# Making the parts of the down weights: spacing, early loads, and the queue of their stores

## The chip, the cores and the metric

The kernel runs on one core of one Trainium2 chip. The metric is the device time of one execution in microseconds (us), the median of several runs. The core has a matrix engine (PE, its weight loads shown as PEld), a vector engine (DVE), a scalar engine (ACT), GpSimd (POOL) and SyncE (SP). SP computes nothing here; it issues transfers. Transfers that POOL issues go through a queue that the profile calls q0 (software_dynamic), those of SP through q1 (hardware_dynamic). All engines take their instructions in order, and wait for each other through semaphores.

## The reference

One transformer block in float32 over 2048 tokens of width 576, with a batch of one:

```
h   = x + attention(layernorm(x))        32 heads of width 18, one shared key and value head
out = h + ((ln(h) Wg) * (ln(h) Wu)) Wd   hidden width 4608, no nonlinearity on either branch

scores = q k^T * 18^-0.5 ; p = softmax(scores) ; o = p v ; attention = o Wo
```

## The kernel before, in words

**Numbers in two parts.** Products are computed to nearly float32 precision from operands that are split into a high part (a cast to a reduced float32 format) and a low part (the rest): three products, high by high, high by low and low by high, are summed in PSUM.

**The stages.** Tokens are taken in four blocks of 512. At first all keys, values and the first queries are made (`keys_values`). Then comes a loop that this document calls the query loop (lines 952 to 962). Each of its steps issues two pairs of score tiles (`pair`: two matmuls on line 500, and one exponential of 128x1024 elements on ACT on line 501), and beside them PE makes the remaining queries of all blocks (`queries`, matmuls on line 337). The rate is 3 units of query work per step; a query of seven heads is 13 units of one and one of four. A head group of four heads takes 16 steps; at its end DVE copies the sums of its values out of PSUM (line 516), and PE can begin the next group's sums only when that bank is empty. The queries of block 0 and their bounds are followed by those of blocks 1 to 3. Each finished query goes through five DVE instructions (lines 344 to 349) and is stored to DRAM through SP (lines 351 and 352); the group after the present one is read back through SP (`prefetch_q`, line 424), from the third tile of a group on.

After the query loop, `steps` goes on with score tiles alone until 208 pairs are made, `load_wo_0` loads and splits the output weights (POOL casts on line 87, DVE subtracts on line 88), block 0 of the residual is loaded, and the first group ends at a guard that all engines pass. The feed-forward part follows, in which later attention runs beside the gate, up and down products.

**The down weights' parts.** The product with the down weights uses seven products of half-size blocks where eight would be needed, and so needs sums of the weights' blocks, each in two parts. `down_weights` makes these once, for 18 pairs of 128-row tiles, and stores them to `wd_dram`; the feed-forward part reads them back many times. It is a generator: the query loop calls it once per step, at the step's end, after `pair`, `run_aux` and `flush`. For a pair p that begins at step `begin(p)`, relative to that step it gives out:

| step | what | engine, line |
|---|---|---|
| -2 | `load`: four blocks, 576 KB | POOL queue, 874 |
| 0 and 1 | `sums`: two subtractions each, 128x288 | POOL, 880 |
| 2 | `high`: two casts, 128x864 and 128x1152 | POOL, 888 |
| 4 and 5 | `low`: one subtraction each, in place | DVE, 894 |
| 6 | `store`: high part and low part, 1008 KB each | POOL queue, 900 |

The last pair (17) has no sums and is stored as it is, in two parts. Within one step, work of a lower pair comes first, and for one pair the order is store, load, sums, high, low.

Each pair lives in a room, two buffers of 128x8x288 elements. Pairs 0 to 9 use two rooms in turn, pairs 10 to 17 three. Rooms come from memory that other tiles have left: the two first residual buffers, the buffer of a block's attention output (pairs 1 and 3), and the normalised inputs of blocks 0 and 1 when their queries are done (`XT0` from pair 5, `XT1` from pair 10). A load waits until the store of the pair that had the room before has landed. The order on every engine is the order of the program text (a manual schedule); a step is a place in that order and not a point in time. An engine whose inputs are there runs ahead of the others.

Pairs 0 to 10 begin six steps apart and the later ones four steps apart:

```
return 2 + 6 * min(p, 10) + 4 * max(p - 10, 0)
```

Of the kernel before, what the change touches and what calls it, by code (L numbers as in the profile page):

```python
# [32 lines left out]
NC = NF // 2  # L33
# [24 lines left out]
class Block:  # L58
# [780 lines left out]
            if not self.half and len(self.pend) > keep:  # L839
                self.flush(len(self.pend) - keep)  # L840

    def steps(self, on):

        while on():
            self.pair()
            self.pair()
            self.run_aux(1)
            self.flush(len(self.pend) - 1)

    def down_weights(self):  # L850

        pool, dve = self.nc.gpsimd, self.dve
        rooms = [(self.hp.tile([P, 8, HD], F32, tag="h", name="wd_src"), self.hp.tile([P, 8, HD], F32R, tag="h", name="wd_hi"))]
        at, where = {}, {}

        def begin(p):
            return 2 + 6 * min(p, 10) + 4 * max(p - 10, 0)  # L860

        def room(p):
            n = p % 2 if p < 10 else (2, 0, 1)[(p - 10) % 3]
            if p in (1, 5, 10):
                home, tag = {1: (self.otp, "oT"), 5: (self.p0q, "XT0"), 10: (self.p0q, "XT1")}[p]
                if p > 1:
                    self.XT[p // 5 - 1] = None
                e = home.tile([P, 9 * TB], F32R, tag=tag, name=f"wd_room{p}").rearrange("p (k j d) -> p k j d", k=2, d=HD)
                rooms[n:] = [(f32(e[:, 0]), e[:, 1])]
            return rooms[n]  # L870

        def load(p):
            where[p] = room(p)
            pool.dma_start(where[p][0][:, 0:4], self.wd[p])

        def sums(p, i):
            src, _ = where[p]
            if p < NC - 1:
                for i, x, y in ((4, 0, 1), (5, 3, 4), (6, 3, 0), (7, 2, 5))[i:i + 2]:
                    pool.tensor_tensor(src[:, i], src[:, x], src[:, y], ALU.subtract)  # L880

        def spans(p):
            return [(1, 4), (4, 8)] if p < NC - 1 else [(0, 4)]

        def high(p):
            src, hi = where[p]
            for lo, to in spans(p):
                pool.tensor_copy(hi[:, lo:to], src[:, lo:to])

        def low(p, i):  # L890

            src, hi = where[p]
            for lo, to in spans(p)[i:i + 1]:
                dve.tensor_tensor(src[:, lo:to], src[:, lo:to], f32(hi[:, lo:to]), ALU.subtract)

        def store(p):
            src, hi = where.pop(p)
            lo, to = spans(p)[0][0], spans(p)[-1][1]
            for k, t in enumerate((f32(hi), src)):
                pool.dma_start(self.wd_dram[p, :, 0:to - lo, k], t[:, lo:to])  # L900
            if p == 3:
                del rooms[1]

        for p in range(NC):
            for d, f in ((6, lambda p=p: store(p)), (-2, lambda p=p: load(p)), (0, lambda p=p: sums(p, 0)), (1, lambda p=p: sums(p, 2)),
                         (2, lambda p=p: high(p)), (4, lambda p=p: low(p, 0)), (5, lambda p=p: low(p, 1))):
                at.setdefault(begin(p) + d, []).append(f)
        for k in range(max(at) + 1):
            for f in at.pop(k, ()):
                f()  # L910
            yield

    def run(self):
        from contextlib import ExitStack
        tc = self.tc
        self.q_dram = tc.dram_tile([NB, H * DH, 3, TB], F32, name="q_dram")
        self.wd_dram = tc.dram_tile([NC, P, 7, 2, HD], F32, name="wd_dram")
        self.wd_list = [(b, p, j) for b in range(NB) for p in range(NC) for j in (range(4) if p == NC - 1 else ORDER)]
        self.n_wd = 0
        self.m_dram = tc.dram_tile([NB, 2, H, TB], F32, name="m_dram")  # L920
        self.known, self.n_mx, self.os, self.chunks = [0] * NB, 0, {}, []
        self.h, self.qt, self.normed, self.wr, self.ws, self.wdo, self.wo_r, self.wos = {}, {}, {}, {}, {}, {}, {}, {}
        self.n_pair, self.half, self.pend, self.aux, self.round = 0, [], [], [], 0
        self.tqs = []
        self.p2, self.p_next, self.wo_from, self.due = None, -1, 10 ** 6, 0.0
        with ExitStack() as st:
            pool = lambda name, bufs, **k: st.enter_context(tc.tile_pool(name=name, bufs=bufs, **k))
            cp, self.lp, self.hp = pool("const", 1), pool("ln", 2), pool("resid", 2)
            self.qp, self.pp, self.op, self.otp = pool("q", 2), pool("P", P_BUFS), pool("o", 1), pool("oT", 1)
            self.ps = pool("ps", 1, space=PSUM)  # L930
            self.C = cp.tile([P, C_W], F32, name="C")
            self.ident = self.C[:, C_ID:C_ID + P]
            self.kT = cp.tile([P, S], F32R, name="kT")
            self.V = cp.tile([P, NT, 32], F32, name="V")
            self.G = cp.tile([P, 64], F32R, name="G")
            self.mx = cp.tile([H, 8], F32, name="mx")
            st.enter_context(tc.manual_schedule())
            with tc.tile_pool(name="p0q", bufs=1) as self.p0q:
                self.wq_h = self.p0q.tile([P, 5, D], F32R, name="wq_h")
                self.wq_l = self.p0q.tile([P, 5, D], F32R, name="wq_l")  # L940
                self.XT = [self.p0q.tile([P, 9, TB], F32R, tag=f"XT{b}", name=f"XT{b}") for b in range(NB)]
                with tc.tile_pool(name="qb", bufs=2) as self.qb:
                    first = self.keys_values()
                    work = self.down_weights()

                    def rest():
                        yield from first
                        for b in range(1, NB):
                            yield from self.queries(b)
                    self.cast = self.dve.tensor_copy  # L950
                    others, live, due = rest(), True, 0.0
                    while live:
                        self.pair()
                        due += RATE
                        while due > 0 and live:
                            z = next(others, None)
                            live = z is not None
                            due -= z or 0
                        self.pair()
                        self.run_aux(1)  # L960
                        self.flush(len(self.pend) - 1)
                        next(work, None)
                    drain(work)
            self.flag()
            self.wp, self.hh, self.p2 = pool("w", 2), pool("hid", 4), pool("P2", 1)
            self.steps(lambda: self.n_pair < WO_FROM)
            self.load_wo_0()
            self.load_x(0)
            self.steps(lambda: self.n_pair % (2 * NT))
            self.flush(len(self.pend))  # L970
            self.guard()
            self.wo_from = self.n_pair + 12
            self.steps(lambda: self.more(0))
            self.cast = self.act.copy
            self.load_w(0)
            self.load_w(1)
            self.load_wd(WD_BUFS - NQ)
            self.load_x(1)
            self.fill(2.0, 1)
            while 0 not in self.normed:  # L980
                self.run_aux(1)
                self.fill(1.0, 1)
            self.split_w(0)
            while self.n_pair % 8 != 4:
                self.pair()
                if not self.half:
                    self.flush(len(self.pend) - 1)
            self.flush(len(self.pend))
            self.normal(0)
            for _ in range(2):  # L990
                self.pair()
            for i, _ in enumerate(self.spread(0)):
                if i % 2 == 0:
                    self.pair()
            self.flush(len(self.pend))
            del self.oT
            self.room()
            self.load_wd(WD_BUFS)
            for b in range(NB):
                self.ffn(b)  # L1000
# [10 lines left out]
WO_FROM = 208  # L1011
# [24 lines left out]
def f32(ap):  # L1036
    return ap.bitcast(F32)
# [10 lines left out]
def drain(gen):  # L1048
    for _ in gen:
        pass  # L1050
# [69 lines left out]
```

## Time and profile before

| what | us |
|---|---|
| median of three runs | 2411.1 |
| lowest and highest | 2410.78, 2415.26 |
| the profiled execution | 2413.92 |
| its span, first to last instruction | 2412.0 |
| PE busy in the span | 2335.0 |
| ACT busy | 1432.2 |
| DVE busy | 1160.4 |
| POOL busy | 669.4 |

The mean granted clock of PE is 0.988 of full speed. A row of the timeline gives the start in us from the span's start, the duration, the engine, the line of the kernel, the operation, the tile written and the tiles read, the shapes and, in brackets, how long the engine was idle before it and what ended that. A row of waits gives the waiting engine and line, the releaser, the total in us, the number of times and the longest. In a row of windows, the stretch and its length stand first, then for PE, PEld, DVE, ACT and POOL the busy time with the number of instructions, and then the granted clock, the busy share of the DMA engines and GB/s.

### The profile page before, as it was taken

Reading aid. Unit: us, or ns where it says so; the run is one execution under the profiler, and the core shown is the slowest. Engines: PE = TensorE matmul, PEld = TensorE weight load, DVE = VectorE, ACT = ScalarE, POOL = GpSimd, SP = SyncE. Lnnn points to the kernel's source line nnn. Section 1 sums busy time; section 2 is a strip of 40 time slices with the busy share of each in tenths; the row PEclk is TensorE's granted clock in tenths of the full one; section 3 lists DMA queues with packets and bytes.
Section 4 is the critical chain, followed back from the end, with each engine's and each line's share of the span. In section 5 each row is a group of like instructions: output and inputs, shape, how many; then the busy total and the mean of one; then the engine's idle time right before and its main releaser. Section 6 shows DMA issues by size and latency. Waiting matters only on the chain.

```text
span 2412.0 us, 46184 instructions
## 1 busy us (share of the span) xinstructions
PE 2335.0 (97%) x18425; PEld 1623.5 (67%) x18425; DVE 1160.4 (48%) x2142; ACT 1432.2 (59%) x1857; POOL 669.4 (28%) x827
## 2 busy tenths in 40 slices
PE   6999888999999999999999999999999999999999
PEld 4434324567677766767767667676766688888887
DVE  7545433444343434543434345443434376566565
ACT  4877666766666666566676766656666623232332
POOL 3655510022222222112222222212221233233332
PEclk9999998999999999999999999999999999999999
DMA  4676752333333333533333333453333344655553
GB/s 138 217 253 224 233 179 92 102 121 108 120 116 121 110 117 104 167 107 116 121 117 121 117 112 111 131 158 116 101 118 108 109 163 163 202 180 190 172 168 119
DMA packets 130467, 340.21 MB, mean 141 GB/s; under 512 B 14760, under 2 KB 15528, under 8 KB 130248
## 3 DMA queue, kind: packets, MB, share of 16 engines
q1 hardware_dynamic: 119208, 290.31, 37.7%
q0 software_dynamic: 11040, 46.89, 5.8%
q8 instruction: 147, 2.41, 0.4%
q14 instruction: 72, 0.59, 0.1%
HBM read 272.63 MB, written 55.67 MB: 136 GB/s over the span
## 4 chain that ended last, share of the span: by engine, by line
PE 81%; DVE 1%; ACT 1%; DMA 1%; issue 0%; SPq 0%; POOL 0%; ACTq 0%; POOLq 0%
PE y L746 17%; PE pg L786 16%; PE acc L505 15%; PE gu L786 12%; PE s L500 9%; PE pu L786 9%; PE yo L616 2%; PE y L734 1%; PE pt L543 1%; ACT P L501 1%; PE to L136 0%; DVE h L749 0%; DMA X<-X 0%; PE tx L665 0%; DMA out_dram<-h 0%
## 5 line engine op out<-in xcount | busy, mean ns | idle before, releaser
L501 ACT ACTIVATE P<-s 128x1024 f32<-128x1024 f32 x1024 | 1030.0, 1027 | 370.8 <-PE s L500 291.1
L786 PE MATMUL pg<-X,ws 64*128 64x512 f32 x2565 | 705.8, 392 | 0.0
L786 PE MATMUL pu<-X,ws 64*128 64x512 f32 x2565 | 705.5, 392 | 0.0
L754 POOL TENSOR_TENSOR h<-h,tmp 128x288 f32<-128x288 f32 x408 | 318.6, 810 | 920.2 <-ACT tmp L753 919.2
L786 PEld LDWEIGHTS pg<-X,ws 64*128 64x128 f32 x2565 | 474.5, 186 | 66.7 <-issue 4.5
L505 PE MATMUL acc<-P,V 128*32 128x512 f32 x4096 | 495.7, 603 | 9.2 <-DVE os L516 8.5
L786 PEld LDWEIGHTS pu<-X,ws 64*128 64x128 f32 x2565 | 472.2, 186 | 31.9
L500 PE MATMUL s<-q,kT 56*128 56x512 f32 x2048 | 440.5, 426 | 14.0 <-DMA q<-q_dram 9.0
L746 PEld LDWEIGHTS y<-wdo,room 128*128 128x128 f32 x2856 | 386.1, 188 | 49.4 <-issue 45.8
L746 PE MATMUL y<-wdo,room 128*128 128x288 f32 x2856 | 404.3, 300 | 1.3 <-DVE h L749 1.2
L753 ACT COPY tmp<-y 128x288 f32<-128x288 f32 x408 | 162.9, 400 | 327.3 <-PE y L746 322.0
L749 DVE TENSOR_TENSOR h<-h,y 128x288 f32<-128x288 f32 x544 | 236.0, 454 | 243.1 <-PE y L746 240.3
L500 PEld LDWEIGHTS s<-q,kT 56*128 56x128 f32 x2048 | 196.1, 186 | 213.0 <-ACT P L501 107.9
L786 PE MATMUL gu<-X,ws 64*128 64x512 f32 x2646 | 309.1, 389 | 0.3 <-DMA X<-X 0.2
L87 POOL CAST ws<-wr 128x1152 fp32r<-128x1152 f32 x144 | 165.8, 1151 | 493.1 <-PE pu L786 239.0
L505 PEld LDWEIGHTS acc<-P,V 128*32 128x32 f32 x4096 | 114.7, 109 | 258.8 <-issue 242.4
L786 PEld LDWEIGHTS gu<-X,ws 64*128 64x128 f32 x2646 | 250.6, 184 | 51.5 <-issue 4.2
L808 DVE TENSOR_TENSOR hf<-pu,g 128x512 f32<-128x512 f32 x95 | 65.7, 692 | 356.1 <-ACT g L804 356.1
L88 DVE TENSOR_TENSOR ws<-wr,ws 128x1152 fp32r<-128x1152 f32 x144 | 194.9, 1353 | 63.6 <-POOL ws L87 63.6
L88 DVE TENSOR_TENSOR room<-S,room 128x1024 fp32r<-128x1024 f32 x68 | 83.3, 1225 | 153.4 <-ACT room L87 153.4
L804 ACT COPY g<-gu 128x512 f32<-128x512 f32 x49 | 28.9, 590 | 138.0 <-PE gu L786 138.0
L87 ACT CAST room<-hf 128x256 fp32r<-128x256 f32 (+1 forms) x144 | 73.9, 513 | 46.6 <-DVE hf L808 46.4
(167 smaller groups left out, 1647.3 us busy)
## 6 DMA issues: line engine op xcount, KB each, us to landing
wdo<-wd_dram SPq DMA_DIRECT2D x492, 288.0 KB
wr<-in_wgu_dram SPq DMA_DIRECT2D x144, 576.0 KB
wd_dram<-wd_room POOLq DMA_DIRECT2D x20, 1008.0 KB, 7.6
q<-q_dram SPq DMA_DIRECT2D x64, 216.0 KB
q_dram<-qs SPq DMA_DIRECT2D x16, 504.0 KB
X<-X SPq DMA_DIRECT2D x28, 256.0 KB
wd_dram<-wd_hi POOLq DMA_DIRECT2D x7, 1008.0 KB, 8.0
wd_dram<-wd_src POOLq DMA_DIRECT2D x7, 1008.0 KB, 8.8
```

The lines of the kernel that those rows point to most:

```text
L87: (copy or self.cast)(hi, src)
L88: self.dve.tensor_tensor(lo, src, f32(hi), ALU.subtract)
L500: self.pe.matmul(s_[:, i], self.kT[o:o + 56, t * P:(t + 1) * P], q[o:o + 56, pr], start=True, stop=True)
L501: self.act.activation(p_, s_, AF.Exp, scale=SCALE)
L505: self.pe.matmul(acc[32 * j:32 * j + 32, :], self.V[:, t, :], Ps[j // 2][:, j % 2, :], start=(t == 0), stop=(t == NT - 1), skip_group_chec ...
L616: pe.matmul(y[:, :HD], m, k, start=(i == 0), stop=(i == len(ms) - 1))
L746: pe.matmul(y[:, :HD], m[:, t * P:(t + 1) * P], k, start=(first and j == 0), stop=(j == 2), skip_group_check=True)
L749: dve.tensor_tensor(hs, hs, y[:, :HD], ALU.add)
L753: act.copy(z, y[:, :HD])
L754: pool.tensor_tensor(hs, hs, z, ALU.add)
L786: pe.matmul(ps, w[o:o + 64, wk, c], X[o:o + 64, xk, c], start=(j == 0), stop=(j == 26))
L808: dve.tensor_tensor(hf, pu, g, ALU.mult)
```

## The change

`begin` starts every pair two steps earlier and leaves five steps, not four, between the pairs after 10. `load` is given out three steps ahead of `begin`, not two, and never before step -1, for which the generator is called once ahead of the loop. `store` issues its two transfers through SP's queue. After pair 16's store the second and third rooms are released. What of the generator is left after the query loop is passed to the following loop of score tiles, and the rest of it is drained after `load_wo_0`.

```diff
-    def steps(self, on):
+    def steps(self, on, work=iter(())):
         while on():
             self.pair()
             self.pair()
             self.run_aux(1)
             self.flush(len(self.pend) - 1)
+            next(work, None)
...
         def begin(p):
-            return 2 + 6 * min(p, 10) + 4 * max(p - 10, 0)
+            return 6 * min(p, 10) + 5 * max(p - 10, 0)
...
             for k, t in enumerate((f32(hi), src)):
-                pool.dma_start(self.wd_dram[p, :, 0:to - lo, k], t[:, lo:to])
-            if p == 3:
-                del rooms[1]
+                sp.dma_start(self.wd_dram[p, :, 0:to - lo, k], t[:, lo:to])
+            if p in (3, NC - 2):
+                del rooms[1:]
...
-            for d, f in ((6, lambda p=p: store(p)), (-2, lambda p=p: load(p)), (0, lambda p=p: sums(p, 0)), (1, lambda p=p: sums(p, 2)),
+            for d, f in ((6, lambda p=p: store(p)), (-3, lambda p=p: load(p)), (0, lambda p=p: sums(p, 0)), (1, lambda p=p: sums(p, 2)),
                          (2, lambda p=p: high(p)), (4, lambda p=p: low(p, 0)), (5, lambda p=p: low(p, 1))):
-                at.setdefault(begin(p) + d, []).append(f)
-        for k in range(max(at) + 1):
+                at.setdefault(max(begin(p) + d, -1), []).append(f)
+        for k in range(-1, max(at) + 1):
...
                     work = self.down_weights()
+                    next(work)
...
                         next(work, None)
-                    drain(work)
             self.flag()
             self.wp, self.hh, self.p2 = pool("w", 2), pool("hid", 4), pool("P2", 1)
-            self.steps(lambda: self.n_pair < WO_FROM)
+            self.steps(lambda: self.n_pair < WO_FROM, work)
             self.load_wo_0()
+            drain(work)
```

More of the change, by code (lines that the diff above doesn't have):

```diff
@@ L848, in steps @@
             self.flush(len(self.pend) - 1)
+            next(work, None)
     def down_weights(self):
-        pool, dve = self.nc.gpsimd, self.dve
+        pool, dve, sp = self.nc.gpsimd, self.dve, self.sp
         rooms = [(self.hp.tile([P, 8, HD], F32, tag="h", name="wd_src"), self.hp.tile([P, 8, HD], F32R, tag="h", name="wd_hi"))]
```

## The prediction, made before the result was known

> **What bounds the kernel now.** I read the page first, then windows over the stage in which the change acts, then the waits of DVE, PE and POOL in the slow part of it, and last the rows in order of time. On the page PE sets the end:
>
> ```profile
> span 2412.0 us, 46184 instructions
> ...
> PE 2335.0 (97%) x18425; PEld 1623.5 (67%) x18425; DVE 1160.4 (48%) x2142; ACT 1432.2 (59%) x1857; POOL 669.4 (28%) x827
> ...
> PE   6999888999999999999999999999999999999999
> ```
>
> 97% busy leaves 77 us. Of the 40 slices of 60.3 us, only the first and the fifth to seventh (241 to 422 us) are under 90% for PE; the down weights' parts are made up to 317 us, so the fifth and most of the sixth are theirs. Windows over that loop (busy time per engine with instruction counts, granted clock, DMA share, GB/s):
>
> ```profile
> 59.90:258.80 198.90, 193.07 (x1402) 79.39 (x1398) 106.35 (x143) 158.34 (x162) 112.60 (x127) 0.97 0.70 230
> 151.00:189.70 38.70, 38.70 (x293) 15.41 (x290) 19.03 (x28) 33.09 (x34) 18.49 (x23) 1.00 0.64 211
> 258.80:332.50 73.70, 57.45 (x361) 23.79 (x359) 31.57 (x46) 39.56 (x40) 31.43 (x38) 0.86 0.71 235
> ```
>
> One step of the loop holds two exponentials on ACT, so the counts give steps: 81 in 198.9 us (2.456 us each), 17 in the undisturbed 38.7 us (2.276), but only 20 in 73.7 us (3.685). At 2.456 the twenty take 49.1 us, so 24.6 us are lost there (28.2 against 2.276). Who waits in those 73.7 us (first three rows PE, then DVE):
>
> ```profile
> PE psq L337 <- DVE qs L344: 11.1, 3, 7.1
> PE acc L505 <- DVE os L516: 4.7, 1, 4.7
> PE psr L337 <- DVE qs L345: 0.5, 2, 0.2
> ...
> DVE wd_room L894 <- POOL wd_room L888: 22.1, 3, 8.3
> DVE wd_src L894 <- POOL wd_hi L888: 10.0, 2, 6.8
> ```
>
> PE waits 16.3 us for DVE, which itself sat 32.1 us in front of the low part's subtraction (line 894) until POOL had cast the high part (line 888). The granted clock of 0.86, if it is full or half, means 0.28 x 73.7 = 20.6 us at half, some 10.3 us lost; 16.3 + 10.3 = 26.6 us confirms the size. One such stall:
>
> ```profile
> 260.67 2.31 POOL L888 CAST wd_room<-wd_room 128x864 fp32r<-128x864 f32 x2
> ...
> 261.93 3.24 DVE L894 TENSOR_TENSOR wd_room<-wd_room 128x864 f32<-128x864 f32 x2 [6.20 <-POOL wd_room L888]
> ...
> 265.09 0.68 DVE L516 COPY os<-acc 128x512 f32<-128x512 f32 x1
> ...
> 265.82 1.94 PE L505 MATMUL acc<-P,V 128*32 128x512 f32 x8 [4.66 <-DVE os L516]
> ```
>
> The copy of the head group's sums is queued on DVE behind the subtraction, and PE needs the bank it empties. POOL is late because its own cycle is longer than the four steps that the plan gives a pair:
>
> ```profile
> 220.42 0.57 POOL L874 DMA_DIRECT2D wd_src<-in_wd_dram  x1
> 224.72 5.10 POOL L880 TENSOR_TENSOR wd_src<-wd_src 128x288 f32<-128x288 f32 x4 [3.73 <-DMA wd_src<-in_wd_dram]
> ...
> 247.79 0.89 POOL L874 DMA_DIRECT2D wd_room<-in_wd_dram  x1
> ...
> 255.99 3.21 POOL L880 TENSOR_TENSOR wd_room<-wd_room 128x288 f32<-128x288 f32 x4 [7.31 <-DMA wd_room<-in_wd_dram]
> 259.15 1.83 POOL L900 DMA_DIRECT2D wd_dram<-wd_room  x2
> 260.67 2.31 POOL L888 CAST wd_room<-wd_room 128x864 fp32r<-128x864 f32 x2
> 262.61 0.88 POOL L874 DMA_DIRECT2D wd_src<-in_wd_dram  x1
> 269.71 3.19 POOL L880 TENSOR_TENSOR wd_src<-wd_src 128x288 f32<-128x288 f32 x4 [6.22 <-DMA wd_src<-in_wd_dram]
> ...
> 304.87 0.86 POOL L874 DMA_DIRECT2D wd_src<-in_wd_dram  x1
> ```
>
> Loads of pairs 13 to 17 start 57.08 us apart in four cycles, 14.3 us each: landing 8.2 (247.79 to 255.99), four sums 3.2, two store issues 1.8, two casts 2.3. Four steps are 4 x 2.276 = 9.1 us. POOL falls behind by 5 us a pair and DVE, then PE, wait for it.
>
> **The change part by part.**
>
> *Spacing 5 for pairs 11 to 17, and stores off POOL.* POOL's order becomes load, sums, casts, next load; the cycle is landing + 3.2 + 2.3 us. The nearest rows for a landing are 4.3 us (220.42 to 224.72) and 8.2 us (247.79 to 255.99). So the cycle is 9.8 to 13.7 us; with a landing of 6.2, the middle, 11.7. The plan now gives 5 x 2.276 = 11.4, or 12.3 at 2.456. I take 6.2: a load still starts about a step after a store, but in another queue.
>
> The Trainium skill, "DMA: Bandwidth & Descriptors", section on queues, rings and completion order, says that each DMA engine takes turns between queues, a packet from each; by that a load no longer waits behind a whole store, the landing is nearer to 4.3, and the full 24.6 us come back. The same page's section on issuing engines says that a second issuing engine saves only the issue time; by that the landing stays and the cycle is 14.3 - 1.8 = 12.5 us, a little too long. No row here has such a load beside stores of another queue.
>
> *Head start at pair 10.* Pair 9 shares two rooms, and its load waits for pair 7's store:
>
> ```profile
> wd_dram<-wd_src POOLq DMA_DIRECT2D x7, 1008.0 KB, 8.8
> ```
>
> Pair 7 begins at step 42; its last subtraction is given out at the end of step 47. Two us for it and the issue and 8.8 to land are 4.7 steps: the load of pair 9 leaves at 52.7, lands 2.7 steps later, sums and casts (5.5 us) take 2.4: 57.8. Pair 10 has the third room, loads then, lands at 60.5, and its first cast ends 3.2 + 1.2 us later, at 62.4. DVE asks for it at the end of step 64: 2.6 steps or 6 us in hand. At 11.7 us a cycle six more pairs use 6 x 0.3 = 1.8 of it: no wait. At 13.7 they use 13.8, so 7.8 us of DVE wait come back; at today's ratio (24.6 lost for 32.1 waited) 6.0 us. So the stage gives 18.6 to 24.6 us; I take 22, since the landing is not known.
>
> *Loads three steps ahead, everything two steps earlier.* POOL has no tie to the steps but through DVE, so the first load stays where it is, behind POOL's earlier work:
>
> ```profile
> 65.71 0.77 POOL L874 DMA_DIRECT2D wd_src<-in_wd_dram  x1
> 70.03 3.39 POOL L880 TENSOR_TENSOR wd_src<-wd_src 128x288 f32<-128x288 f32 x4 [3.55 <-DMA wd_src<-in_wd_dram]
> 73.37 2.92 POOL L888 CAST wd_hi<-wd_src 128x864 fp32r<-128x864 f32 x2
> ```
>
> Its first cast ends at about 74.7, and DVE will ask for it at the end of step 4, 59.9 + 5 x 2.456 = 72.2: up to 2.5 us of wait, beside scores that go on; nothing. In the six-step part a subtraction moves against the group ends (every 16 steps) by two steps. PE's only waits on DVE before 258.8 are these:
>
> ```profile
> PE acc L505 <- DVE os L516: 3.8, 2, 3.0
> PE to L136 <- DVE ob L552: 2.0, 1, 2.0
> ```
>
> So that part can gain 5.8 us or, with the order unlucky, lose as much: I take 0 and keep both ends. POOL's waits in front of line 900 there vanish, but hide nothing that PE waits for.
>
> *Stores through SP.* 36 issues (two for each of 18 pairs, 0.9 us each on POOL) move. SP gets them behind query stores and ahead of the next prefetch of q, and now waits for DVE's subtraction with those behind it. The nearest prefetch rows, on SP:
>
> ```profile
> 267.52 0.75 SPq L424 DMA_DIRECT2D q<-q_dram  x2
> ...
> 319.81 2.25 SPq L424 DMA_DIRECT2D q<-q_dram  x2
> ```
>
> A prefetch is issued two steps into a group and needed at the next group's start, 14 steps or 32 us later; a store that holds SP for a step and takes 8.8 us to land fits. Query tiles have two buffers, 5.7 steps (13 us) to the next query: that holds too. Cost 0, with the DMA side in a rival.
>
> *Last pair, room release, work passed to the scores' loop.* The loop runs on while queries are left. They yield 327 units, 3 a step: 110 steps, 220 pairs, over the 208 at which the scores' loop stops. The rows agree, queries ending at 343.7 us while pair 17 now ends near 317:
>
> ```profile
> L337 PE MATMUL psq<-XT,wq_l x95: 384/392/628, 60.3 to 343.7; 64*126 64x512 f32 x75, 64*72 64x512 f32 x20
> ...
> 315.84 0.76 POOL L900 DMA_DIRECT2D wd_dram<-wd_src  x1 [0.59 <-DVE wd_src L894]
> ```
>
> Pair 17 will be stored at step 101, still inside the query loop. The added argument of the scores' loop and the later drain do nothing, the last pair stays beside queries, and the release after pair 16 frees rooms that nobody needs before step 110. Cost 0.
>
> **The sum.** -22 + 0 + 0. The profiled execution took 2413.92 us (2412.0 of span), so 2391.9 for it; it lies 2.8 us above the median 2411.1, on which I forecast 2389 us. Behind the loop PE works in program order and is at 90% or more from the eighth slice on, so time won before stays won unless a wait right behind the loop grows (third rival).
>
> **The rivals.**
>
> *POOL still binds.* Landing stays 8.2 and the head start is gone as well: seven pairs slip by 13.7 - 11.4 = 2.3, 16 us of DVE wait, 12.4 us lost at today's ratio. Gain 12: 2399 us. For it: the DMA share is 0.71 in the slow part although POOL takes 14.3 us a pair; a faster pair raises it. Against: two stores no longer stand before the load in its queue.
>
> *Slower: SP's queue carries the stores row by row.* Page, part 3:
>
> ```profile
> q1 hardware_dynamic: 119208, 290.31, 37.7%
> q0 software_dynamic: 11040, 46.89, 5.8%
> ...
> q_dram<-qs SPq DMA_DIRECT2D x16, 504.0 KB
> ...
> q_dram<-qs SPq DMA_DIRECT2D x16, 252.0 KB
> ```
>
> POOL's queue moved 4.25 KB a packet in 203 ns (5.8% of 16 x 2412 us over 11040), though a stored row is 1152 bytes, so it packs rows; SP's moved 2.44 KB in 122 ns. A pair's two stores are 1792 rows. Bounded above by 122 ns a row, they take 13.7 us on 16 engines; with the load (576 KB, 139 packets of 203 ns, 1.8) and a query's stores (756 KB at 2.44 KB in 122 ns, 2.4) that is 17.9 us a pair, 322 us for 18, against 272.6 us (59.9 to 332.5) today: 2411 + 49 = 2460 us. It decides from 272.6 / 18 = 15.1 us a pair. A line through both queues' points gives 13 ns + 45 ns per KB, 65 ns a row, 7.2 us, 11.4 a pair: no loss. I hold to the line.
>
> The skill's page on DMA puts the size below which a transfer loses its rate, in its specifications, at 512 bytes; by that the rows cost nothing extra, and no run here shows it.
>
> *No change: the stall moves behind the loop.* Output weights are loaded into the freed rooms:
>
> ```profile
> POOL wo L87 <- PE acc L505: 42.6, 1, 42.6
> ```
>
> POOL is idle for 42.6 us before them, so after a store's landing of 8.8 and a load's of 4.3 pair 17 has some 29 us. The plan uses 5 steps (11.4) of it. Only if the chain ended 40 us behind the plan would the 22 be gone: 2411. Nothing in the rows says so.
>
> **How the numbers follow.** Forecast 0.55 (its own range 2381 to 2398: 24.6 + 5.8 and 18.6 - 5.8 off), POOL still binds 0.24 (2393 to 2405), better than both 0.04 (28.2 + 5.8: 2377), no change 0.08, slower 0.09. A measurement of this kernel tells about 0.2%, 5 us, from no change. So faster 0.83, same 0.08, slower 0.09. The range 2380 to 2404 leaves out the last two and the edges.
>
> **What would show it.** Right: in the windows, steps 81 to 101 at 2.3 to 2.6 us each and a clock near 0.97; the waits of L894 for L888 under 10 us in all; POOL's loads 11 to 12 us apart from pair 12 on, landing in 5 to 7 us; lines 616 and after unchanged but shifted. Wrong: POOL's sums still waiting 7 us for their loads; POOL's loads waiting for stores to land (SP's queue slow); PE waiting for q at a group's start; or new waits of DVE for POOL in steps 0 to 81.

## The result, and the profile after

The changed kernel takes 2385.0 us (median of four runs; 2382.8 to 2386.3) against 2411.1 us before: ratio 0.9887, 95% interval 0.987 to 0.9904. That is 26 us less, where 22 were forecast. The profiled execution is one of 2382.75 us with a span of 2381.0 us.

The page of the changed kernel: span, busy time, PE's slices, and the two queues (packets, MB, share of 16 engines):

```profile
span 2381.0 us, 46227 instructions
...
PE 2320.0 (97%) x18425; PEld 1615.3 (68%) x18425; DVE 1152.1 (48%) x2142; ACT 1430.9 (60%) x1857; POOL 640.0 (27%) x791
...
PE   5999989999999999999999999999999999999999
...
q1 hardware_dynamic: 151272, 326.59, 42.7%
q0 software_dynamic: 2592, 10.62, 1.6%
```

PE executes the same 18425 matmuls. Beside the first, only the sixth slice (298 to 357 us) is now under 90%, and it holds the stall behind the query loop. The same three kinds of windows as before: steps 0 to 81, the undisturbed 17 steps, and the 20 steps (81 to 101) in which the kernel before lost its time:

```profile
61.00:257.30 196.30, 191.26 (x1402) 78.82 (x1398) 102.83 (x145) 157.98 (x162) 96.20 (x106) 0.98 0.75 243
151.00:189.70 38.70, 38.70 (x293) 15.41 (x290) 17.66 (x28) 33.04 (x34) 17.13 (x20) 1.00 0.72 240
257.30:306.80 49.50, 48.89 (x361) 20.74 (x359) 27.50 (x44) 39.06 (x40) 19.06 (x23) 1.00 0.88 284
```

Again 40 exponentials and 361 matmuls in the last row, so the same work: 49.5 us where it was 73.7. The clock there is 1.00, was 0.86. PE's and DVE's waits in those 20 steps:

```profile
PE acc L505 <- DVE os L516: 0.4, 1, 0.4
PE psr L337 <- DVE qs L345: 0.2, 1, 0.2
...
DVE wd_room L895 <- POOL wd_room L889: 5.9, 1, 5.9
```

PE's 16.3 us of waiting for DVE are 0.6, DVE's 32.1 us for POOL are 5.9 (the lines of the parts are one higher in the changed kernel). Where the 26 us lie, by the start of each step's first exponential in the two traces: steps 0 to 60 took 147.2 us and take 146.0, 60 to 81 51.8 and 50.3, 81 to 101 73.8 and 49.6, 101 to 110 21.4 both times, 110 to 120 36.0 and 35.1, 120 to 140 59.5 both times. So 24.2 of the loop's 26.8 us lie in one stage. The two profiled executions differ by 31 us because they fell to different sides of their medians; the 26 us are the medians'.

### The profile page after: what moved, and what is told of

It is laid out like the page before. It is cut to its first block, busy times and chain, and to the rows that moved or that the text cites. A ratio compares the mean times of both kernels' runs of the same rounds, so it can differ in the third digit from the quotient of the medians.

```text
span 2381.0 us, 46227 instructions
## 1 busy us (share of the span) xinstructions
PE 2320.0 (97%) x18425; PEld 1615.3 (68%) x18425; DVE 1152.1 (48%) x2142; ACT 1430.9 (60%) x1857; POOL 640.0 (27%) x791
## 3 DMA queue, kind: packets, MB, share of 16 engines
q1 hardware_dynamic: 151272, 326.59, 42.7%
## 4 chain that ended last, share of the span: by engine, by line
PE 82%; DVE 1%; ACT 1%; DMA 1%; issue 0%; SPq 0%; ACTq 0%; DVEq 0%
PE y L746 17%; PE pg L786 17%; PE acc L505 15%; PE gu L786 12%; PE s L500 9%; PE pu L786 8%; PE yo L616 3%; PE y L734 1%; PE pt L543 1%; ACT P L501 1%; PE to L136 0%; PE tx L665 0%; DVE h L749 0%; DMA X<-X 0%; DMA out_dram<-h 0%
## 5 line engine op out<-in xcount | busy, mean ns | idle before, releaser
L500 PE MATMUL s<-q,kT 56*128 56x512 f32 x2048 | 436.7, 423 | 13.6 <-DVEq L390 8.6
```

The costliest lines, as they stand in the source:

```text
L500: self.pe.matmul(s_[:, i], self.kT[o:o + 56, t * P:(t + 1) * P], q[o:o + 56, pr], start=True, stop=True)
```

## Experiments

The theory tested is the prediction's: PE loses time where POOL's cycle for a pair is longer than the steps that the plan gives it, since DVE then waits for POOL, and PE for DVE. Rivals are that the queue alone matters, that the spacing alone matters, and that the place of DVE's wait decides and not its length.

**Spacing alone.**

```diff
-            return 2 + 6 * min(p, 10) + 4 * max(p - 10, 0)
+            return 2 + 6 * min(p, 10) + 5 * max(p - 10, 0)
```

> The kernel before with the five-step spacing alone; stores stay in POOL's queue, pairs begin two steps later than in the change. Theory of POOL's cycle (its cycle with store issues, 14.3 us, against 5 x 2.276 = 11.4 us): seven pairs slip 2.9 us each, 20 us, less 6 us of head start, 14 us of DVE wait, 11 us lost of 24.6, so about 2397 us. Rival, the queue (a load lands late because it stands behind two stores in POOL's queue): nothing changes, 2406 to 2411. Rival, spacing alone does it: 2385.

Measured: 2392.7 us (ratio to before 0.9925, 0.9909 to 0.9942), 18.6 us of the 26. The window of steps 81 to 101:

```profile
258.80:312.90 54.10, 50.47 (x361) 21.31 (x359) 29.75 (x45) 39.14 (x40) 31.07 (x37) 0.97 0.86 287
```

And DVE's waits for POOL in the same stretch:

```profile
DVE wd_room L894 <- POOL wd_room L888: 11.0, 2, 6.2
DVE wd_src L894 <- POOL wd_hi L888: 7.3, 1, 7.3
```

The theory's direction holds, its price does not: DVE still waits 18.3 us for POOL, which at the prediction's ratio (24.6 for 32.1) is 14 us lost, yet the twenty steps are only 5 us over the 49.1 that the prediction took for a stage without loss. A wait of DVE is not paid at a fixed ratio. What fits is a rate. POOL's loads of pairs 12 to 17 start 13.6 us apart here; over five steps a pair that is 2.72 us a step, and 20 steps took 54.1 us, 2.71 each. In the kernel before, 14.3 us over four steps is 3.58 a step, and the rows gave 3.69. While DVE waits for POOL pair after pair, the loop runs at POOL's cycle divided by the spacing, or at PE's own pace of some 2.4 us a step where that is longer.

While DVE waits at every pair the two quotients have to agree, whichever engine sets the pace. That it is POOL is read from what POOL itself waits for. In the 73.7 us of the kernel before, this was its own loads for 24.2 us, and DVE for 1.7:

```profile
POOL wd_room L880 <- DMA wd_room<-in_wd_dram: 13.6, 2, 7.2
POOL wd_src L880 <- DMA wd_src<-in_wd_dram: 6.2, 1, 6.2
POOL wd_hi L888 <- DMA wd_src<-in_wd_dram: 4.4, 1, 4.4
POOL wd_dram L900 <- DVE wd_room L894: 1.1, 1, 1.1
POOL wd_dram L900 <- DVE wd_src L894: 0.6, 1, 0.6
```

**Stores through SP alone.**

```diff
-                pool.dma_start(self.wd_dram[p, :, 0:to - lo, k], t[:, lo:to])
+                sp.dma_start(self.wd_dram[p, :, 0:to - lo, k], t[:, lo:to])
```

> The kernel before with the stores on SP alone; four steps between pairs, pairs begin as before. Theory of POOL's cycle: 13.7 us a pair, as between the loads of pairs 12 and 17 in the changed kernel, against 9.1: 4.6 x 7 less 6 is 26 us of DVE wait, 20 us lost, a gain of 4 to 8 us, 2403 to 2407. Rival, the queue: 2385 to 2390. Rival, spacing alone: 2411.

Measured: 2397.6 us (0.9941, 0.9925 to 0.9958), a gain of 14 us, between the two theories' numbers. The windows of steps 0 to 60 and 81 to 101:

```profile
60.30:213.60 153.30, 146.97 (x1039) 60.41 (x1038) 81.14 (x107) 117.42 (x120) 67.30 (x78) 0.95 0.69 221
263.80:323.70 59.90, 53.19 (x361) 22.59 (x359) 31.66 (x46) 39.22 (x40) 21.17 (x25) 0.91 0.81 265
```

POOL's loads of pairs 12 and 17, which bound five cycles:

```profile
238.83 0.57 POOL L874 DMA_DIRECT2D wd_room<-in_wd_dram  x1
...
297.70 0.57 POOL L874 DMA_DIRECT2D wd_src<-in_wd_dram  x1
```

58.9 us for five cycles is 11.8 us each: this is what POOL takes when nothing but its own chain holds it, and it is the prediction's 11.7. The 13.7 in the expectation above was read from the changed kernel, where POOL stands idle for more than its own chain, and was the wrong number. 11.8 over four steps is 2.94 a step; the 20 steps took 3.00 each.

What the move took out of the cycle is mainly POOL's issues, and less surely the landing. For pairs 12 to 16 the mean from a pair's first sum to the next load is 5.5 us here, against 6.8 in the kernel before and 7.1 with the spacing alone, where POOL issues the stores in between; from the load to the first sum it is 6.3 here, against 7.5 and 6.5.

DVE's waits for POOL in the 20 steps:

```profile
DVE wd_room L894 <- POOL wd_room L888: 12.9, 3, 5.0
...
DVE wd_src L894 <- POOL wd_hi L888: 6.5, 2, 5.8
```

That is 19.4 us, about as long as the 18.3 with the spacing alone, but the stage lost 10.9 us here and 5 there: once more no fixed price. Neither the spacing nor the queue is the whole cause: each alone removes most of the loss (19.7 and 13.8 us in the 20 steps) and together they remove 24.2, since both shorten the same excess. The first 60 steps, however, took 6 us longer than before the change in the profiled execution, which lies 3 us over its median; the next run says why.

**The change without its earlier start.**

```diff
-            return 6 * min(p, 10) + 5 * max(p - 10, 0)
+            return 2 + 6 * min(p, 10) + 5 * max(p - 10, 0)
```

> The changed kernel with every pair two steps later (as before the change), five-step spacing and SP stores kept. Theory: the place of DVE's subtractions against the group ends is worth under 3 us either way, 2382 to 2388. Rival, the earlier start is what leaves POOL its head start: waits of line 895 for line 889 come back, 2392 or more.

Measured: 2388.1 us (2385.1 to 2391.9; 0.9904, 0.9888 to 0.9921). The 20 steps are as in the changed kernel (49.3 us), but steps 0 to 60 take 150.6 us and not 146.0. One place, in order of time:

```profile
195.79 1.99 POOL L889 CAST wd_hi<-wd_src 128x864 fp32r<-128x864 f32 x2
196.73 1.97 DVE L895 TENSOR_TENSOR wd_src<-wd_src,wd_hi 128x864 f32<-128x864 f32 x1 [4.12 <-POOL wd_hi L889]
198.62 0.68 DVE L344 COPY qs<-psr 126x512 f32<-126x512 f32 x1
199.35 0.50 PE L337 MATMUL psq<-XT,wq_h 64*126 64x512 f32 x1 [1.74 <-DVE qs L344]
```

Here DVE's wait stands in front of the copies at a query's end, PE needs the banks that they empty, and a stretch of half clock (3.4 us) follows. The run with stores on SP alone has the same place and waits there too. So the two steps by which every pair begins earlier are worth some 3 us once the stores are on SP; the interval of this run and that of the changed kernel overlap, so the 3 us rest on the profiles' 4.6 us in one stage more than on the times.

**The change with the stores back in POOL's queue.** PE, DVE and ACT have the changed kernel's instructions in its order.

```diff
-                sp.dma_start(self.wd_dram[p, :, 0:to - lo, k], t[:, lo:to])
+                pool.dma_start(self.wd_dram[p, :, 0:to - lo, k], t[:, lo:to])
```

> The changed kernel with the stores back in POOL's queue. PE, DVE and ACT have the same instructions in the same order as the changed kernel. Theory of POOL's cycle: as the run with the spacing alone, about 2397. Rival, the queue of the stores only moves issue time and POOL has room for it: 2385 to 2388. Rival, the stores in front of the loads are the whole cause: 2406 or more.

Measured: 2393.8 us (0.9926, 0.9909 to 0.9942), as with the spacing alone. The stores' queue is worth 9 us beside the spacing. POOL's loads are 14.3 us apart again; steps 60 to 81 take 54.8 us (50.3 in the changed kernel) and 81 to 101 52.7, or 2.64 a step. The rate, 14.3 / 5 = 2.86, does not give this number: DVE waited for POOL only once in the loop, for 8.7 us, and not pair after pair. PE lost its time at two places from step 60 on, 5.2 us in front of line 136, a transposition of what DVE has just written (2.1 in the changed kernel), and 1.8 in front of line 337, each with 3.4 us of half clock after it.

**Loads on SP too**, so that they share the stores' queue again, with PE, DVE and ACT unchanged in order.

```diff
-            pool.dma_start(where[p][0][:, 0:4], self.wd[p])
+            sp.dma_start(where[p][0][:, 0:4], self.wd[p])
```

> The changed kernel with the loads on SP as well, so that loads and stores share a queue again; PE, DVE and ACT keep their order. Theory that the load's place behind stores in one queue costs: landing of the loads back at 7 to 9 us in nearly all pairs, a few waits of DVE for POOL, 2387 to 2396, in part because SP waits for rooms in front of query stores. Rival, all transfers share the engines and the queue is indifferent: landing as in the changed kernel (3.9 to 9.0 us), 2383 to 2387.

Measured: 2389.2 us (2387.6 to 2391.0; 0.9904, 0.9887 to 0.9921), 4 us over the changed kernel. One load behind two stores on SP, and the sums that wait for it on POOL:

```profile
246.60 2.69 SPq L901 DMA_DIRECT2D wd_dram<-wd_room  x2
249.34 2.49 SPq L875 DMA_DIRECT2D wd_src<-in_wd_dram  x1
...
260.18 4.32 POOL L881 TENSOR_TENSOR wd_src<-wd_src 128x288 f32<-128x288 f32 x4 [2.82 <-DVE wd_room L895]
```

10.8 us from issue to sums here, and a mean of 9.1 for pairs 12 to 16, against 6.3 in the changed kernel (3.9, 8.9, 4.1, 9.0 and 5.7). In steps 60 to 81, which took 53.9 us against 50.3, PE waited 4.2 us in front of line 136, where it waited 2.1 in the changed kernel.

This does not show that a queue of its own makes a load land sooner. With loads and stores together in POOL's queue the same mean was 7.5 us in the kernel before, 6.5 with the spacing alone and 7.0 with the stores back; with the two apart it was 6.3 with SP alone, 6.3 in the changed kernel and 7.3 without its earlier start. What the packets in the traces show is how close in time the load stands behind the stores. In this run the loads of pairs 12, 14, 16 and 17, right behind two stores in SP's queue, had their first packet 6.2 to 6.5 us after their issue. Loads of pairs 11 to 17 in a queue of their own that were issued within some 4 us of two stores still had theirs after 3.8 to 5.4 us (seven loads in five of the kernels with stores on SP), and those issued 8 us or more behind the last store after 1.3 to 2.5. The Trainium skill, "DMA: Bandwidth & Descriptors", section on queues, rings and completion order, has the engines take turns between queues, a packet from each; the late first packets do not agree with that for stores issued just ahead of the load, and why is not known.

**Six steps between all pairs.**

```diff
-            return 6 * min(p, 10) + 5 * max(p - 10, 0)
+            return 6 * p
```

> The changed kernel with six steps between all pairs (the last store at step 108 of 110). Theory of POOL's cycle: the changed kernel's 13.7 us between loads already costs PE almost nothing, so nothing is left to win in the loop: 2382 to 2387, with no wait of line 895 for line 889. Rival, POOL still costs PE at five steps: 2375 to 2380. Rival, the chain's later end delays the output weights behind the loop: 2390 or more.

Measured: 2385.2 us (0.9887, 0.987 to 0.9903), the changed kernel's time. DVE's waits for POOL fall to 1.8 us in the loop and nothing is won, as the rate has it: past 2.4 us a step PE sets the pace. A chain that ends at step 108 delays nothing behind the loop either.

**Four steps, and three, with the rest of the change kept.**

```diff
-            return 6 * min(p, 10) + 5 * max(p - 10, 0)
+            return 6 * min(p, 10) + 4 * max(p - 10, 0)
```

> The changed kernel with four steps between the pairs after 10. Rate law (when DVE waits for POOL pair after pair, a step takes POOL's cycle divided by the spacing: before 14.3 / 4 = 3.6, spacing alone 13.6 / 5 = 2.7, SP alone 11.8 / 4 = 2.9 us, each as measured): seven pairs at 11.8 us are 83 us against 28 steps x 2.4 = 67, 16 us, less the 6 to 10 us of head start that the earlier begin leaves: 6 to 10 us slower than the changed kernel, 2391 to 2395. Rival, spacing is not needed once the stores are off POOL: 2384 to 2387.

Measured: 2394.8 us (0.9932, 0.9915 to 0.9949), 9.8 us over the changed kernel, inside the 6 to 10 of the rate. POOL's loads of pairs 13 to 17 are 11.3 us apart, 2.82 a step, and steps 81 to 101 took 2.85 each. With four steps the load also stands elsewhere in POOL's order, ahead of the casts of the pair before it, and with three, below, between that pair's sums; so these are not quite the chain that the 11.8 was measured on.

```diff
-            return 6 * min(p, 10) + 5 * max(p - 10, 0)
+            return 6 * min(p, 10) + 3 * max(p - 10, 0)
```

> The changed kernel with three steps between the pairs after 10. Rate law: 11.8 / 3 = 3.9 us a step over the 21 steps of seven pairs, 83 us against 50, 33 us, less 6 to 10 us of head start: 23 to 27 us slower than the changed kernel, 2408 to 2412, as slow as before. Rival, a wait of DVE costs only where PE needs what is queued behind it, at a few group and query ends: 2392 to 2400.

Measured: 2409.4 us (0.9993, 0.9984 to 1.0003): the whole gain is gone by the spacing alone, 24.4 us over the changed kernel, with 23 to 27 expected. Sixteen steps (70 to 86) of this kernel:

```profile
234.50:297.20 62.70, 46.78 (x283) 17.77 (x281) 36.36 (x36) 31.67 (x32) 31.44 (x34) 0.82 0.78 258
```

What POOL waited for between steps 60 and 101:

```profile
POOL wd_room L875 <- DMA wd_dram<-wd_room: 25.5, 2, 15.7
POOL wd_src L875 <- DMA wd_dram<-wd_src: 6.6, 1, 6.6
```

62.7 us for 16 steps is 3.92 a step, the law's number, but POOL's cycle is not what it was in the law: 32 us of POOL's time go to waiting for a room, that is for a store to land. At three steps (and once, 12.3 us, at four) the three rooms limit, not the chain of load, sums and casts. The loads of pairs 13 to 17 are 12.0 us apart. That this lies beside the 11.8 of the law is luck as far as this run shows: the law's size came out, but which resource sets the cycle had changed.

**The copy of a group's sums on ACT, in the kernel before.**

```diff
-                self.dve.tensor_copy(os_, self.acc)
+                (self.act.copy if b == 0 and g < NG - 1 else self.dve.tensor_copy)(os_, self.acc)
```

> The kernel before with one edit: the copy of a head group's sums runs on ACT, not DVE, in the groups of the query loop, so that it can't stand behind DVE's subtraction. DVE still waits for POOL as before. Theory that DVE's wait costs only where PE needs what is queued behind it (the group's sums: 8.5 us of PE's waits; the end of a query: 11.1 us): the first of the two goes, 8 to 13 us with the half clock after it, 2398 to 2403. Rival, DVE's wait costs by its length wherever it stands: 2408 to 2411.

Measured: 2405.1 us (0.9968, 0.9955 to 0.998), 7 us under the kernel before and between the two ranges expected. PE's waits for that copy are gone, and the slow stage is as slow as before. Steps 0 to 60 and 81 to 101:

```profile
60.10:202.50 142.40, 142.39 (x1040) 58.74 (x1038) 79.19 (x104) 118.18 (x123) 83.92 (x95) 0.98 0.71 238
254.30:327.40 73.10, 57.58 (x363) 23.84 (x359) 30.24 (x44) 40.28 (x42) 31.55 (x38) 0.86 0.71 237
```

PE's waits for DVE in the 20 steps, both over 1 us:

```profile
PE psq L337 <- DVE qs L344: 12.2, 3, 7.8
PE pt L543 <- DVE m L88: 3.1, 1, 3.1
```

The 20 steps took 73.1 us (73.8 before): with one way from DVE to PE removed, PE waits nearly as long at others, 15.5 us in all where it was 16.3, most of it at the ends of queries. That is what a rate does, and not what single collisions do. Of the 7 us that the run gains, 4.8 lie in steps 0 to 60 (142.4 us against 147.2), where PE is now busy throughout: there the copy's place did cost, by collision.

**Output weights split after the guard, on the changed kernel.**

```diff
+    def split_wo_0(self):
+        rs = self.wo_rs
         for c in range(5):
             self.split(self.wo_0[:, 0, c], self.wo_0[:, 1, c], rs[c // 2][:, c % 2], self.nc.gpsimd.tensor_copy)
...
             self.guard()
+            self.split_wo_0()
```

> The changed kernel with one edit outside the change: the output weights are loaded where they were but split after the guard, so that the copy of a group's sums is not queued on DVE behind the five subtractions of the split. Behind the loop PE now stands for some 9 us (the copy runs at 339.9 us, 6 us of which DVE waited for POOL and 5 us subtracted). Theory: the copy runs as soon as the sums are there, 5 to 9 us come back, 2376 to 2380. Rival, the guard itself takes the time: 2385.

Measured: 2382.8 us (2381.3 to 2383.9; 0.9876, 0.986 to 0.9893), 2 us under the changed kernel, with intervals that overlap, and nearer to the rival. The copy and the first matmul behind the guard, in the changed kernel:

```profile
339.27 0.68 DVE L516 COPY os<-acc 128x512 f32<-128x512 f32 x1
...
341.88 1.22 PE L500 MATMUL s<-q,kT 56*128 56x512 f32 x4 [8.64 <-DVEq L390]
```

And with the edit:

```profile
333.44 0.69 DVE L516 COPY os<-acc 128x512 f32<-128x512 f32 x1 [5.07 <-PE acc L505]
...
340.13 1.22 PE L500 MATMUL s<-q,kT 56*128 56x512 f32 x4 [6.74 <-SPq L390]
```

The copy runs 5.8 us earlier, but PE starts again only 1.8 us earlier: where 1.9 us passed between the copy's end and the matmul, 6.0 us do now, at the guard. What else the guard waits for was not tried.

**Both edits on the changed kernel** (the copy on ACT, the split after the guard).

> The changed kernel with two edits outside it: the output weights are split after the guard, and in the query loop's groups the copy of a group's sums runs on ACT. In the kernel before that copy's move shortened steps 0 to 60 by 4.8 us. Expected: 4 to 7 us under the changed kernel, 2378 to 2381. Rival, the copy on ACT only delays the next exponentials: 2383 to 2387.

Measured: 2377.1 us (2376.0 to 2379.3; 0.9859, 0.9843 to 0.9876): 8 us under the changed kernel, and under both ranges expected. Steps 0 to 60 take 141.5 us in it with PE busy for all of them:

```profile
60.70:202.20 141.50, 141.48 (x1040) 58.68 (x1038) 80.39 (x105) 118.15 (x123) 69.09 (x82) 0.99 0.77 248
```

## Why the prediction was right, point by point

*What bounds, and the sum.* Right. The stage was to go from 73.7 to between 49.1 and 55.1 us and went to 49.5. The forecast of 22 had kept back 2.6 us for a landing that might be late; the stage gave 24.2. The other 2.6 us of the loop's gain lie ahead of the stage, where the sum had 0.

*POOL's cycle.* Right in its size: 11.7 us were put for a landing of 6.2, and the landings of pairs 12 to 16 had a mean of 6.3; with stores on SP alone the cycle was 11.8. In part this is luck. The 6.2 was the middle of two rows, only one of the five landings (5.7) lies in the 5 to 7 us that were to show it, and two sums waited 8.4 us for their load, over the 7 that were named as a sign of being wrong. The parts listed for the kernel before (8.2, 3.2, 1.8 and 2.3) add up to 15.5 and not to 14.3, since the landing shown was longer than the mean, 7.5, and the issues overlap other work. Of the two rules between which the landing was left open, 9.8 us by a landing of 4.3 and 12.5 by the issues saved alone, the 11.8 lies nearer to the second.

Wrong in what would show it: loads 11 to 12 us apart were expected in the changed kernel, and they are 13.7 apart (222.41 to 291.09 for five). POOL is no longer the one that others wait for at every pair, and itself waits for its inputs and, it seems, once for a room. The load of pair 13 stood 7.3 us. The row puts that down to DVE; but its room was last used by pair 10, whose stores SP issued only at 228.80, behind a prefetch, and with four and three steps the same load stands 12.3 and 15.7 us by rows that name a store out of a room. A load that waits for a store to land was another of the signs of being wrong:

```profile
222.41 0.57 POOL L875 DMA_DIRECT2D wd_room<-in_wd_dram  x1
...
240.69 0.57 POOL L875 DMA_DIRECT2D wd_room<-in_wd_dram  x1 [7.34 <-DVE qs L347]
249.62 3.20 POOL L881 TENSOR_TENSOR wd_room<-wd_room 128x288 f32<-128x288 f32 x4 [8.36 <-DMA wd_room<-in_wd_dram]
...
291.09 0.57 POOL L875 DMA_DIRECT2D wd_src<-in_wd_dram  x1
```

*The head start at pair 10.* Right, and larger than worked out. The first cast of pair 10 was to end at step 62.4, 6 us before DVE asks for it; it ended in step 61, and DVE took it up 10 us later. But it was to last for all pairs, and by pair 16 it was gone: there DVE waited the 5.9 us shown above.

*The price of a wait.* The step that failed. "Today's ratio (24.6 lost for 32.1 waited)" turned DVE's waits into lost time, and gave the lower end of the stage and the first rival's 2399. With the spacing alone DVE waited 18.3 us in the stage, 14 us by the ratio, and the stage lost 5. In its place stands the rate: POOL's cycle over the spacing, where that exceeds PE's own 2.4 us a step. It fits the kernel before, the spacing alone, SP alone and four steps, each within 0.11 us a step. It does not describe the stores back in POOL's queue, where DVE waited once only, and in the three-step run the cycle was set by rooms, so the law says how a cycle is paid and not what sets it. What is lost in the end can be added up from PE alone: its waits for DVE in the 20 steps, and half of the time that the clock records give at half speed. That is 16.3 + 10.2 us in the kernel before (24.6 lost), 3.6 + 1.7 with the spacing alone (5.0) and 6.7 + 5.1 with SP alone (10.9). The sum was not hurt, and that is luck: with a landing of 6.2 there was no wait to price, and the 5.9 us that did come would be 4.5 lost by the ratio, where PE's waits for DVE were 0.6 in all.

*Everything two steps earlier.* Taken as 0 with 5.8 us either way; the run without it is 3 us slower, in the six-step part, by a wait in front of a query's end. Inside the bounds, and a gain that belongs to the change: the stores on SP alone cost 6 us in the first 60 steps at the old begin.

*Loads three steps ahead; the last pair, the releases, the later drain.* The loads' step is a place in the program's order and POOL has nothing between the two places; put back to two, every engine has the same instructions in the same order, and the same holds when the last pair's parts are drained ahead of the scores' loop and the rooms released as before. In the changed kernel the last query matmul starts at 318.1 us:

```profile
L337 PE MATMUL psq<-XT,wq_l x95: 384/391/625, 61.4 to 318.1; 64*126 64x512 f32 x75, 64*72 64x512 f32 x20
```

Pair 17's last store is issued by SP before that:

```profile
309.95 1.19 SPq L901 DMA_DIRECT2D wd_dram<-wd_src  x1
```

The last pair does not run beside scores alone, as the count of 110 steps said.

*The rivals.* The slower one fell on the page: SP's queue does carry the stores row by row (32064 packets more), but their share rose from 37.7% to 42.7% of 16 engines, 1718 us, or 54 ns a row, under the line's 65 and far from the 122 that were its upper bound. The Trainium skill, "DMA: Bandwidth & Descriptors", specifications, puts the size for full rate at 512 bytes; rows of 1152 bytes here agree. The stall behind the loop stayed what it was (36.0 and 35.1 us for steps 110 to 120), so nothing was handed back there.

## What to carry to other kernels

Where one engine prepares data for another in a fixed rotation and a third runs in order behind the second, compare cycles and not waits: as long as the second engine waits at every turn, the loop runs at the slower of its own step and the helper's cycle divided by the steps it is given, and a wait that the helper's rate allows for costs little. What sets the helper's cycle (its own chain, or buffers that come free late) is read from the helper's own waits. Shortening the helper's cycle and giving it more steps buy the same microseconds, so their gains do not add. What is left after that are collisions at single places (a copy that frees a bank, queued behind something late), and these are moved by a step or two of the plan, or by giving the copy to another engine.

## What was not expected of the hardware

A load in a queue of its own still took 8.9 and 9.0 us in two of five pairs, beside 3.9 and 4.1 in two others, with stores in flight on SP's queue; issued within some 4 us of two stores in the other queue, a load had its first packet 3.8 to 5.4 us after its issue, against 1.3 at best. A row of 1152 bytes costs SP's queue 54 ns as a packet of its own, while POOL's queue moved packets of 4.25 KB on the mean in 203 ns, which is 47 and 48 ns per KB: packing rows bought nothing here. And with the copy out of the way, the guard behind the loop still kept PE for 6 us.
